# Normalised tokens of eleven chunks: written to DRAM as a high part, with the low part added there by a second transfer, in place of a sum formed on GpSimd

## The chip, the cores and the metric

The kernel runs as one program on one core of one Trainium2 chip. The metric is device time in microseconds (us): the median over timed runs. Engines are called by the names of the profile: PE is TensorE (matmuls), DVE VectorE, ACT ScalarE, POOL GpSimd, SP SyncE, which here only issues transfers. Each engine works through its own instructions strictly in the order of the program. They wait for each other by semaphores, and a waiting instruction holds up everything behind it on its engine.

## What is computed

Three stages, all in fp32. Attention over 8 x 8 heads of 576 tokens and 64 dimensions gives x (8 x 576 x 512). A layer norm and a two-layer MLP with a residual follow, then a mixing stage along channels and tokens. The change lies in what connects the first two:

```python
kv = np.einsum('bhsf,bhsd->bhfd', k_p, v)
num = np.einsum('bhsf,bhfd->bhsd', q_p, kv)
...
x = np.ascontiguousarray(attn_out.transpose(0, 2, 1, 3)).reshape(B, S, H * D)
xn = (x - mu) / np.sqrt(var + 1e-06) * g_ln
ch = np.maximum(xn @ w_ch1, 0.0) @ w_ch2        # 512 -> 2048 -> 512
x = x + ch
```

## The kernel before

**Split products.** A product in fp32 is made of three matmuls: each operand is cut into a high part, which PE takes as it is, and a low part, the rest (`mm3`, L73 to L76: L74 high by high, L75 low by high, L76 high by low). High parts are made on ACT (`hi_act`, L61), low parts on DVE (`lo_vec`, L64) or POOL (`lo_pool`, L67).

**Attention and the first MLP part run interleaved.** Attention is 16 units (4 pairs of batches by 4 pairs of heads). For a group of tokens of a unit PE projects keys or queries (`pj`), DVE takes the row maximum (`m`, L304) and subtracts it (`ys`, L306), PE turns the tile over (`tr`, L381), ACT takes exponentials (`pf`) and cuts the high part (`kph`, `qp`), DVE makes the low part of keys (`kpl`, L64), and POOL that of queries (`qp`, L67; in the last unit DVE). PE accumulates `kv` from `kph`, `kpl` and the values `vh`, `vl`, and makes the numerators `nm` from `qp` and `kv`. ACT copies them out (`num`, L420), PE turns them over (L433), and DVE divides (`rd`, L436 and L437; `xo`, L439) and collects the statistics of the norm (`lst`, L444). When the four units of a pair of batches are done, `ln_final` (L231 to L242) gives the mean and the factor of each token.

Finished tokens go through the first MLP part, `mlp_a`: 512 of the 2048 hidden features, in 18 chunks of 256 tokens. `tokens(ch)` loads the two tiles of 128 tokens (L507) and normalises each (`xn`, DVE L518). PE turns it over (L522), ACT cuts the high part `xh` and DVE the low part `xl`. POOL then adds the two to `xt` (L529), and SP stores `xt` to `xn_d[ch]` in DRAM (L530). PE goes on from `xh` and `xl`: 24 matmuls `ph<-xh,w` and `ph<-xl,w` (up, 128x256), ACT and DVE make the hidden tiles `hh`, `hl` (L206, L207), and 24 matmuls `ph<-w,hh` and `ph<-w,hl` (down, 128x512) end in a DVE sum with the residual (L557) and a store (L558). The later three quarters of the hidden features ("B" rounds, from 640 us on) read the normalised tokens back from `xn_d`.

A chunk is **wide** from the twelfth on (number 11; numbers begin at 0): attention is at its end by then, its PSUM tiles `nm` and `tr` are free for the transposes, ACT takes over the normalising (L516) and copies `xt` out of PSUM itself (L527). So POOL's sums stand in chunks 0 to 10 alone: 11 chunks, 22 sums of 128x512. `xn`, `xh`, `xl` and `xt` have one buffer each in these chunks, so the first tile of a chunk waits until the last reader of the chunk before is done. The second normalised tile of a chunk and the first of the next are made one behind the other.

**What sets the order.** The code is written as generators that are advanced in turn, with priorities for parts of it. A scheduler that keeps a simulated timeline then puts the instructions of each engine in a row: an instruction taken out or put in can shift the rows around it, and far from it. During the first two stages SP issues all transfers in one queue, in the order of the rows.

Of the kernel before, what the change touches and what calls it, by code (L numbers as in the profile page):

```python
# [9 lines left out]
F32 = mybir.dt.float32  # L10
# [5 lines left out]
ALU = mybir.AluOpType  # L16
# [4 lines left out]
P = 128  # L21
# [8 lines left out]
KC = DM // P  # L30
# [8 lines left out]
NC_ = CT * P  # L39
# [8 lines left out]
def f32(ap):  # L48
    return ap.bitcast(F32)
# [3 lines left out]
def body(ctx, tc, qT, kT, va, wbd, g, w1, w2, wth, wtok, wch, out):  # L53
    nc = tc.nc
    V, A, G, T, SY = nc.vector, nc.scalar, nc.gpsimd, nc.tensor, nc.sync
# [4 lines left out]
    def hi_act(dst, src):  # L60
        A.activation(dst, src, AF.Copy)  # L61

    def lo_vec(dst, src, hi):
        V.tensor_tensor(dst, src, f32(hi), op=ALU.subtract)  # L64
# [13 lines left out]
    def opened(*a, **kw):  # L78
        st = ExitStack()
        return st, st.enter_context(tc.tile_pool(*a, reuse_waits="tile", **kw))  # L80
# [4 lines left out]
    xn_d = [dram.tile([P, KC, NC_], F32, name=f"xnd{c}") for c in range(NCH)]  # L85
# [402 lines left out]
    def mlp_a(m):  # L488
        nonlocal chunk

        def wide(ch):
            return tail is not None and ch >= tail + WIDE

        def transposed(ch, i):
            if not wide(ch):
                return ps_ph.tile([P, KC, P], F32, name="ph")
            return (ps_tr if i % 2 else ps_nm).tile([P, KC, P], F32, name="tr" if i % 2 else "nm")

        def tokens(ch):
            x = []  # L500
            for i in range(CT):
                p, t = divmod(ch * CT + i, NT)
                if wide(ch) and ch % 3 == 1:
                    x.append(p_mt.tile([P, DM], F32, name=f"x{i}"))
                else:
                    x.append(p_ma.tile([P, DM], F32, name="x", bufs=XB))
                SY.dma_start(out=x[i], in_=x_d[p][:, t, :])  # L507
            pool = p_ma if not wide(ch) or ch % 2 else p_mt
            xh = pool.tile([P, KC, NC_], F32R, name="xh")
            xl = pool.tile([P, KC, NC_], F32R, name="xl")  # L510
            xt = p_ma.tile([P, KC, NC_], F32, name="xt")
            for i in range(CT):
                xn = p_ma.tile([P, DM], F32, name="xn")
                p, t = divmod(ch * CT + i, NT)
                if wide(ch):
                    A.activation(xn, x[i], AF.Identity, scale=ln_rs[p][:, t:t + 1], bias=ln_nb[p][:, t:t + 1])  # L516
                else:
                    V.tensor_scalar(xn, x[i], ln_mv[p][:, t, 0:1], ln_rs[p][:, t:t + 1], op0=ALU.subtract,  # L518
                                    op1=ALU.mult)
                tp = transposed(ch, i)  # L520
                for c in range(KC):
                    T.transpose(tp[:, c, :], xn[:, c * P:(c + 1) * P], ident)  # L522
                o = slice(i * P, (i + 1) * P)
                hi_act(xh[:, :, o], tp)
                lo_vec(xl[:, :, o], tp, xh[:, :, o])
                if wide(ch):
                    A.activation(xt[:, :, o], tp, AF.Copy)  # L527
                else:
                    G.tensor_tensor(xt[:, :, o], f32(xh[:, :, o]), f32(xl[:, :, o]), op=ALU.add)  # L529
            SY.dma_start(out=xn_d[ch], in_=xt)  # L530
            return x, xh, xl

        nxt = None
        for ch in range(NCH):
            if nxt is None:
                yield ch
                chunk = ch
                nxt = tokens(ch)
            x, xh, xl = nxt
            nxt = None  # L540
            yield -1
            hid = []
            for f in range(m.nf // 2):
                if wide(ch) and f % 2:
                    ph = ps_pj.tile([P, 2, NC_], F32, name="pj")
                else:
                    ph = ps_ph.tile([P, 2, NC_], F32, name="ph")
                m.up(f, ph, xh, xl)
                hid.append(m.relu(p_ma, ph))
                yield -1  # L550
                if f == 0 and ch + 1 < NCH and wide(ch):
                    nxt = tokens(ch + 1)
                    yield -1
            for i in range(CT):
                acc = ps_ph.tile([P, DM], F32, name="ph")
                m.down(i, acc, hid)
                V.tensor_tensor(x[i], acc, x[i], op=ALU.add)  # L557
                SY.dma_start(out=xp_d[ch][:, i, :], in_=x[i])  # L558
                yield -1
# [8 lines left out]
    done, msteps, p_ma, p_mt, need, tail, chunk = 0, 0, None, None, 0, None, 0  # L568
    for g in ga:
# [5 lines left out]
        if done >= nload:  # L575
            if p_ma is None:
                s_st.close()
                s_ma, p_ma = opened(name="ma", bufs=1, side="left")
# [74 lines left out]
    def load_b(ch, xt=None):  # L653
        if xt is None:
            xt = p_xb.tile([P, KC, 4 * P], F32, name="xt")
        for i in range(2):
            SY.dma_start(out=xt[:, :, i * NC_:(i + 1) * NC_], in_=xn_d[2 * ch + i])
        return xt
# [35 lines left out]
    xt = load_b(0, first[:, 0:4].rearrange("p k a c -> p k (a c)"))  # L694
# [458 lines left out]
    for r in range(2):  # L1153
        done = 0
        for ch in range(NQ):
# [7 lines left out]
            for n, m in enumerate(ms):  # L1163
# [9 lines left out]
                if r == 0 and ch == 0 and n == 1:  # L1173
                    xt = load_b(1)
# [4 lines left out]
                if n == len(ms) - 1 and not (r and last):  # L1179
# [5 lines left out]
                    if not (r and ch == NQ - 2):  # L1185
                        xt = load_b((ch + 2) % NQ)
# [204 lines left out]
```

## Time and profile before

| what | value |
|---|---|
| median of 3 runs | 1669.17 us (1665.57 to 1670.7) |
| the profiled execution | 1668.41 us |
| its span | 1666.6 us |
| PE busy | 1619.8 us (97%) |
| DVE busy | 1279.9 us (77%) |
| ACT busy | 876.3 us (53%) |
| POOL busy | 721.7 us (43%) |
| mean granted PE clock | 0.99 of full speed |

The profile is one execution. "Busy" is the time in which an engine had an instruction in work. A timeline row gives the start, the busy time, engine, line, operation, what is written from what, how many in a row, and in brackets the idle time ahead of it and what ended that. Matmuls overlap in the pipe, so the distance of their starts says more than the busy time of one: at full clock 0.119 us for 256 columns. The granted clock is given in shares of the full 2.4 GHz; half of it is the other level, 1.2 GHz. Idle time on an engine other than PE costs something only where PE ends up waiting for it.

### The profile page before, as it was taken

The page shows a single profiled execution, that of the slowest core. Times are in us where ns is not written, and L with a number is a line of the kernel's source. Part 1 is how long each engine was busy: PE and PEld are TensorE (multiplying, and loading weights), DVE is VectorE, ACT ScalarE, POOL GpSimd, SP SyncE. Part 2 cuts the span into 40 slices and gives each one's busy share as a digit, 9 for nine tenths or more (in the row PEclk, how much of TensorE's full clock was granted, in tenths as well). Part 3 has the DMA queues.
Part 4 walks back from the last instruction along what each step waited for, and adds up shares of the span by engine and source line. Part 5 has one row for each costly group of instructions (what it writes and reads, how often), then busy time and mean ns, then how long its engine had stood idle before and what let it go on. Part 6 is the DMA issues. An engine that isn't in the chain of part 4 may idle for free.

```text
span 1666.6 us, 29023 instructions
## 1 busy us (share of the span) xinstructions
PE 1619.8 (97%) x11080; PEld 1487.9 (89%) x11080; DVE 1279.9 (77%) x2277; ACT 876.3 (53%) x1715; POOL 721.7 (43%) x562
## 2 busy tenths in 40 slices
PE   8899999999999999999999999999998999999998
PEld 6777899999999888889899999998898899999998
DVE  7989878888987953778786676688666787888884
ACT  6777767677775652445453444444443444444441
POOL 7876988899981001222112222211322443344430
PEclk9999999999999999999999999999999999999999
DMA  5334333333322734455547444463257565865754
GB/s 190 102 95 126 110 96 105 114 111 109 112 77 88 243 123 152 150 173 194 191 166 267 168 154 153 135 226 129 87 209 281 176 233 207 279 216 206 241 201 178
DMA packets 120329, 273.81 MB, mean 164 GB/s; under 512 B 9088, under 2 KB 62720, under 8 KB 112768
## 3 DMA queue, kind: packets, MB, share of 16 engines
q1 hardware_dynamic: 119904, 270.93, 47.9%
q8 instruction: 87, 1.43, 0.3%
q10 hardware_dynamic: 288, 1.05, 0.2%
q14 instruction: 50, 0.41, 0.1%
HBM read 195.92 MB, written 73.92 MB: 162 GB/s over the span
## 4 chain that ended last, share of the span: by engine, by line
PE 83%; DVE 11%; issue 2%; DMA 2%; POOL 1%; ACT 1%; SPq 0%; DVEq 0%; ACTq 0%; POOLq 0%
PE acc L74 6%; PE acc L75 6%; PE acc L76 6%; PE ph L75 4%; PE ph L76 4%; PE ph L74 4%; PE pa L74 3%; PE pa L76 3%; PE pa L75 3%; PE mc L74 2%; PE mc L75 2%; PE mc L76 2%; PE pj L74 2%; PE ma L74 2%; PE ma L76 2%; PE ma L75 2%
## 5 line engine op out<-in xcount | busy, mean ns | idle before, releaser
L667 POOL TENSOR_TENSOR c<-xt 128x512 f32<-128x512 f32 x17 | 22.7, 1335 | 373.8 <-DMA xt<-xnd 273.4
L74 PE MATMUL acc<-wd,hb 128*128 128x512 f32 x432 | 170.2, 394 | 1.8 <-DVE xo L833 1.8
L75 PE MATMUL acc<-wd,hb 128*128 128x512 f32 x432 | 170.1, 394 | 0.0
L67 POOL TENSOR_TENSOR qp<-pf,qp 128x512 fp32r<-128x512 f32 (+1 forms) x120 | 147.8, 1255 | 13.4 <-ACT qp L61 12.8
L76 PE MATMUL acc<-wd,hb 128*128 128x512 f32 x432 | 152.6, 394 | 0.4 <-DVE hb L787 0.4
L304 DVE TENSOR_REDUCE m<-pj 128x4 f32<-128x512 f32 (+1 forms) x160 | 99.4, 625 | 40.0 <-PE pj L76 39.4
L64 DVE TENSOR_TENSOR kpl<-pf,kph 128x1024 fp32r<-128x1024 f32 (+1 forms) x67 | 100.6, 1501 | 11.1 <-ACT kph L61 10.8
L64 DVE TENSOR_TENSOR a<-zf,a 128x1024 fp32r<-128x1024 f32 (+1 forms) x57 | 97.7, 1724 | 12.0 <-ACT a L61 11.9
L306 DVE TENSOR_TENSOR ys<-pj,m 128x512 f32<-128x512 f32 (+1 forms) x160 | 99.6, 628 | 2.1 <-ACT qf L391 0.5
L316 ACT ACTIVATE pf<-ys 128x512 f32<-128x512 f32 (+1 forms) x160 | 85.3, 584 | 30.2 <-DVE ys L306 23.2
L61 ACT ACTIVATE a<-zf 128x1024 fp32r<-128x1024 f32 (+1 forms) x57 | 56.7, 1013 | 82.8 <-POOL zf L927 40.2
L74 PEld LDWEIGHTS acc<-wd,hb 128*128 128x128 f32 x432 | 81.7, 189 | 13.7 <-DVE xo L833 2.4
L75 PE MATMUL kv<-kpl,vh 128*65 128x256 f32 x300 | 86.2, 287 | 7.2 <-DVE kpl L64 7.2
L75 PEld LDWEIGHTS acc<-wd,hb 128*128 128x128 f32 x432 | 81.7, 189 | 10.9
L76 PEld LDWEIGHTS acc<-wd,hb 128*128 128x128 f32 x432 | 77.5, 189 | 13.0 <-DVE hb L787 1.1
L74 PE MATMUL kv<-kph,vh 128*65 128x256 f32 x300 | 86.4, 288 | 0.0
L76 PE MATMUL kv<-kph,vl 128*65 128x256 f32 x300 | 84.5, 282 | 0.0
L780 ACT ACTIVATE u<-pa 128x256 f32<-128x256 f32 x108 | 41.2, 382 | 71.1 <-PE pa L76 70.3
L1090 POOL TENSOR_SCALAR k<-k 128x512 f32<-128x512 f32 x31 | 27.5, 888 | 114.1 <-ACT k L1089 114.1
L420 ACT ACTIVATE num<-nm 65x288 f32<-65x288 f32 x128 | 50.6, 402 | 49.6 <-PE nm L76 42.5
L74 PE MATMUL ma<-t,a 128*128 128x288 f32 x248 | 74.5, 301 | 1.9 <-ACT a L61 1.9
L76 PE MATMUL ma<-t,a 128*128 128x288 f32 x248 | 73.7, 300 | 1.3 <-DVE a L64 1.3
(402 smaller groups left out, 6308.3 us busy)
## 6 DMA issues: line engine op xcount, KB each, us to landing
t<-wtkdt SPq DMA_DIRECT2D x16, 1440.0 KB, 7.3
t<-wtkd SPq DMA_DIRECT2D x15, 1440.0 KB, 6.2
t<-wtkdt SPq DMA_DIRECT2D x16, 1152.0 KB, 6.6
xt<-xnd SPq DMA_DIRECT2D x34, 512.0 KB, 5.0
raw<-in_w SPq DMA_DIRECT2D x32, 512.0 KB, 4.3
in<-in_va SPq DMA_DIRECT2D x30, 325.0 KB, 3.1
xd<-xo SPq DMA_DIRECT2D x48, 192.0 KB, 3.0
x<-xd SPq DMA_DIRECT2D x36, 256.0 KB, 3.0
```

The costliest lines, as they stand in the source:

```text
L61: A.activation(dst, src, AF.Copy)
L64: V.tensor_tensor(dst, src, f32(hi), op=ALU.subtract)
L67: G.tensor_tensor(dst, src, f32(hi), op=ALU.subtract)
L74: T.matmul(out_, lhsT=lh, rhs=rh, start=start, stop=False, **kw)
L75: T.matmul(out_, lhsT=lh, rhs=rl, start=False, stop=False, **kw)
L76: T.matmul(out_, lhsT=ll, rhs=rh, start=False, stop=stop, **kw)
L304: V.tensor_reduce(m[:, :2 * n], pv, axis=AX.X, op=ALU.max, apply_absolute_value=True)
L306: marks.append(V.tensor_tensor(ys[:, :2 * n, :], pv, m[:, :2 * n].unsqueeze(2).to_broadcast([P, 2 * n, NF]), op=ALU.subtract).ins)
L316: A.activation(kp[:, :2 * n, s, :], ys[:, :2 * n, :], AF.Exp, scale=sc)
L420: A.activation(self.num[:, h, o:o + 288], nm, AF.Copy)
L780: A.activation(t, ps, AF.Copy)
L1090: G.tensor_scalar(k, k, -MAGIC, 1.0, op0=ALU.add, op1=ALU.mult)
```

## The change

In chunks 0 to 10 the tile `xt` and its two POOL sums are gone. SP stores `xh` to `xn_d[ch]`, and POOL then issues a transfer of `xl` to the same place which adds to what lies there. The wide chunks keep `xt`. Lines behind the diff move by one to two (the residual sum is L559 then, the new store L531, the accumulating transfer L532).

```diff
-            xt = p_ma.tile([P, KC, NC_], F32, name="xt")
+            xt = p_ma.tile([P, KC, NC_], F32, name="xt") if wide(ch) else None
...
                 lo_vec(xl[:, :, o], tp, xh[:, :, o])
                 if wide(ch):
                     A.activation(xt[:, :, o], tp, AF.Copy)
-                else:
-                    G.tensor_tensor(xt[:, :, o], f32(xh[:, :, o]), f32(xl[:, :, o]), op=ALU.add)
-            SY.dma_start(out=xn_d[ch], in_=xt)
+            if wide(ch):
+                SY.dma_start(out=xn_d[ch], in_=xt)
+            else:
+                SY.dma_start(out=xn_d[ch], in_=f32(xh))
+                G.dma_start(out=xn_d[ch], in_=f32(xl), accum_op=ALU.add)
```

The accumulating transfer waits for the store (a semaphore of SP's queue, `DMAHW`) and for DVE's `xl`. The next chunk's `xh` waits for the store, and its first `xl` for the accumulating transfer (`DMASW`), since both read the one buffer. The loads of `xn_d` for the B rounds wait for it too.

The change also moves rows on all engines up to the end of the first MLP part, since the scheduler places them anew; from 640 us on the order is the same in both kernels. Three places follow.

**DVE, chunk 10, the last one ahead of the wide chunks.** The rows `xs` are the B rounds' first operands, made from `xn_d`; names in brackets are the semaphores waited for. Before:

```order
L518 TENSOR_SCALAR xn<-x,lmv,lrs 128x512 [waits DMAHW7_49,PE_49]
L242 SCALAR_TENSOR_TENSOR lnb<-lmv,lrs 128x9 [waits DVE_49]
L64 TENSOR_TENSOR xl<-ph,xh 128x4x128 [waits Activation_49]
L64 TENSOR_TENSOR xs<-xs 128x512 [waits DMAHW6_49,Activation_49]
L667 TENSOR_TENSOR xs<-xs 128x512 [waits DMAHW7_49]
L672 TENSOR_TENSOR xs<-xs 128x512
L64 TENSOR_TENSOR xs<-xs 128x512 [waits Activation_49]
L64 TENSOR_TENSOR xl<-ph,xh 128x4x128 [waits Activation_49]
```

After:

```order
L518 TENSOR_SCALAR xn<-x,lmv,lrs 128x512 [waits DMAHW5_49,PE_49]
L64 TENSOR_TENSOR xl<-ph,xh 128x4x128 [waits DMASW1_49,Activation_49]
L436 TENSOR_SCALAR rd<-kv 128x6 [waits PE_49]
L437 RECIPROCAL rd<-rd 128x6 [waits DVE_49]
L439 TENSOR_TENSOR xo<-kv,rd 128x384 [waits DMAHW2_49,DVE_49]
L64 TENSOR_TENSOR xl<-ph,xh 128x4x128 [waits Activation_49]
```

The `xs` rows stood between the two `xl` of the chunk; now they come behind the `xl` of chunk 11, and a short piece of a division stands there.

**PE, chunk 9.** Each row of four transposes `ph<-ident,xn` is one of the chunk's two tiles; `nm<-qp` are the last unit's numerators. Before:

```order
L433 MATMUL kv<-ident,num 128x65
L522 MATMUL ph<-ident,xn 128x128 x4
L433 MATMUL nm<-ident,num 128x65
L74 MATMUL nm<-qp_7606,kvh 65x288
L75 MATMUL nm<-qp_7607,kvh 65x288
L76 MATMUL nm<-qp_7606,kvl 65x288
...
L433 MATMUL kv<-ident,num 128x65
L522 MATMUL ph<-ident,xn 128x128 x4
```

After:

```order
L522 MATMUL ph<-ident,xn 128x128 [waits DVE_49]
L522 MATMUL ph<-ident,xn 128x128 x3
L381 MATMUL tr<-ident,ys 128x128 [waits PE_49,Activation_49]
L381 MATMUL tr<-ident,ys 128x128 x3
L433 MATMUL nm<-ident,num 128x65 [waits Activation_49]
L433 MATMUL nm<-ident,num 128x65 x5
L381 MATMUL tr<-ident,ys 128x128 [waits DVE_49,PE_49,Activation_49]
L381 MATMUL tr<-ident,ys 128x128 x3
L522 MATMUL ph<-ident,xn 128x128 [waits DVE_49]
L522 MATMUL ph<-ident,xn 128x128 x3
L355 MATMUL nm<-ident,kvs 128x65 [waits DVE_49]
L74 MATMUL ph<-xh,w_0_0_0_162 128x256 [waits DVE_49,Activation_49]
```

Before, six of the numerators stood between the two tiles and 18 more between the second tile and the second matmul of the up products. Now chunk 9 is brought ahead of the numerators, and transposes alone lie between its first tile and its up products.

**DVE, chunk 8.** Before:

```order
L518 TENSOR_SCALAR xn<-x,lmv,lrs 128x512
L436 TENSOR_SCALAR rd<-nm 128x6
L64 TENSOR_TENSOR xl<-ph,xh 128x4x128
L64 TENSOR_TENSOR kvl<-nm,kvh 128x260
L437 RECIPROCAL rd<-rd 128x6
L304 TENSOR_REDUCE m<-pj 128x4
L439 TENSOR_TENSOR xo<-nm,rd 128x384
L306 TENSOR_TENSOR ys<-pj,m 128x512
```

After:

```order
L64 TENSOR_TENSOR xl<-ph,xh 128x4x128
L437 RECIPROCAL rd<-rd 128x6
L439 TENSOR_TENSOR xo<-nm,rd 128x384
L304 TENSOR_REDUCE m<-pj 128x4
L444 BN_STATS lst<-xo 128x6 x3
L518 TENSOR_SCALAR xn<-x,lmv,lrs 128x512
L306 TENSOR_TENSOR ys<-pj,m 128x512
L436 TENSOR_SCALAR rd<-nm 128x6
L64 TENSOR_TENSOR kpl<-pf,kph 128x1024
L64 TENSOR_TENSOR xl<-ph,xh 128x4x128
```

The second form is nearly the one that chunk 1 has in both kernels, on DVE and on PE: a division, its statistics, both tiles of the norm and a `kpl` of 128x1024 lie in one run.

## Rows read from the trace of the kernel before

**Rows 1.** Windows: time, length, busy us of PE, PEld, DVE, ACT, POOL; clock, DMA.

```profile
350.00:400.00 50.00, 48.87 (x395) 47.14 (x394) 41.61 (x71) 36.86 (x70) 46.94 (x40) 1.00 0.34 101
...
500.00:560.00 60.00, 56.15 (x411) 52.48 (x410) 48.46 (x113) 30.53 (x57) 8.38 (x6) 0.94 0.43 146
```

**Rows 2.** Windows of 5 us at the two long stops of PE.

```profile
210.00:215.00 5.00, 5.00 (x27) 5.00 (x27) 4.71 (x11) 0.00 (x0) 5.00 (x7) 0.57 0.13 45
550.00:555.00 5.00, 3.84 (x18) 3.85 (x19) 5.00 (x7) 1.77 (x3) 1.67 (x1) 0.50 1.05 407
```

**Rows 3.** Waits of PE, 160 to 560 us: total us, times, longest.

```profile
PE kv L75 <- DVE kpl L64: 5.1, 5, 2.4
```

**Rows 4.** Groups of POOL, 160 to 560 us: busy us, mean ns of one, idle before.

```profile
L529 POOL TENSOR_TENSOR xt<-xh,xl 128x512 f32<-128x512 f32 x22 | 33.3, 1518 | 46.2 <-DVE xl L64 46.1
```

**Rows 5.** The store's line L530 (issue in ns, time to landing), and another transfer.

```profile
L530 SPq DMA_DIRECT2D xnd<-xt x18: 319/323/424, 168.5 to 636.3; - x18
DMA to landing us min/median/max: 2.6/2.7/5.5
...
wch<-wcd SPq DMA_DIRECT2D x4, 512.0 KB, 10.5
```

**Rows 6.** Timeline of PE, chunk 1.

```profile
205.84 0.36 PE L74 MATMUL ph<-xh,w 128*128 128x256 f32 x1 [0.61 <-DVE xl L64]
...
206.90 0.35 PE L74 MATMUL pj<-wb,kh 128*128 128x256 f32 x1 [0.70 <-DVE ys L306]
...
209.93 0.47 PE L75 MATMUL kv<-kpl,vh 128*65 128x256 f32 x1 [2.44 <-DVE kpl L64]
...
214.26 0.31 PE L75 MATMUL ph<-xl,w 128*128 128x256 f32 x1
```

**Rows 7.** Timeline of DVE, chunk 1.

```profile
198.33 1.84 DVE L64 TENSOR_TENSOR kpl<-pf,kph 128x1024 fp32r<-128x1024 f32 x1
...
200.70 0.67 DVE L557 TENSOR_TENSOR x<-ph,x 128x512 f32<-128x512 f32 x1
...
207.34 2.54 DVE L64 TENSOR_TENSOR kpl<-pf,kph 128x1024 fp32r<-128x1024 f32 x1
```

**Rows 8.** Timeline of PE, chunk 10.

```profile
546.18 0.66 PE L522 MATMUL ph<-ident,xn 128*128 128x128 f32 x4 [0.88 <-DVE xn L518]
547.92 0.39 PE L74 MATMUL ph<-xh,w 128*128 128x256 f32 x1 [1.08 <-ACT xh L61]
548.62 0.96 PE L522 MATMUL nm<-ident,xn 128*128 128x128 f32 x4 [0.32 <-ACT xn L516]
551.16 0.58 PE L75 MATMUL ph<-xl,w 128*128 128x256 f32 x1 [1.57 <-DVE xl L64]
```

**Rows 9.** Timeline of DVE, chunk 10.

```profile
546.89 1.80 DVE L64 TENSOR_TENSOR xs<-xs 128x512 fp32r<-128x512 f32 x1
...
550.43 0.68 DVE L64 TENSOR_TENSOR xl<-ph,xh 128x512 fp32r<-128x512 f32 x1
```

**Rows 10.** Durations: timelines of ACT and PE, and a group of DVE.

```profile
502.18 1.09 ACT L395 ACTIVATE pf<-tr 128x512 f32<-128x512 f32 x2 [0.63 <-PE tr L381]
...
504.20 1.05 ACT L61 ACTIVATE qp<-pf 128x1024 fp32r<-128x1024 f32 x1
...
506.09 0.60 ACT L61 ACTIVATE xh<-ph 128x512 fp32r<-128x512 f32 x1
...
528.18 0.61 PE L522 MATMUL ph<-ident,xn 128*128 128x128 f32 x4
...
L64 DVE TENSOR_TENSOR qp<-pf,qp 128x1024 fp32r<-128x1024 f32 x4 | 5.6, 1400 | 1.0 <-ACT qp L61 1.0
```

**Rows 11.** Timeline of PE, chunk 5.

```profile
381.80 0.34 PE L75 MATMUL kv<-kpl,vh 128*65 128x256 f32 x1 [1.13 <-DVE kpl L64]
```

**Rows 12.** Timelines of POOL and of SP, chunk 2.

```profile
257.31 2.57 POOL L67 TENSOR_TENSOR qp<-pf,qp 128x512 fp32r<-128x512 f32 x2 [0.41 <-DMA x<-xd]
...
256.93 0.32 SPq L530 DMA_DIRECT2D xnd<-xt  x1
```

## Prediction

> **What bounds the kernel now.** I read the page first (PE is busy 97% of the span), then PE by stages, then what PE waits for in the stage that the change touches, then the timelines at those waits. From 160 us to the end of the first MLP part at 640 us PE runs without a break except in short stops; the window of 350 to 400 us holds 1.13 us of them, that of 500 to 560 us 3.85 us [rows 1]. What ends PE's waits in this stage is DVE above all, `kpl` first [rows 3]; no wait of PE in the stage ends on POOL. So POOL's sums, 22 of them for 33.3 us [rows 4], are off the path. What the change can move is the two long stops, and others that a new order may make.
>
> Stop 1 is in chunk 1: 0.61 + 0.70 + 2.44 = 3.75 us idle, the last of it for a `kpl` that took 2.54 us [rows 6, 7]. After it PE is slow for a while: the granted clock of 210 to 215 us is 0.57, against 1.00 over a stretch like 350 to 400 us [rows 1]; half is the lower of its two levels, 1.2 GHz [rows 2]. Twenty matmuls from 209.93 to 214.26 us take 4.33 us [rows 6], where they would take 20 x 0.119 = 2.4 us at full clock: 1.9 us more. Together 5.65 us. Stop 2 is in chunk 10: 0.88 + 1.08 + 0.32 + 1.57 = 3.85 us idle [rows 8], and again a stretch at half clock, 0.50 [rows 2], for the 20 matmuls that follow; the same 1.9 us, together 5.75 us. Its reason is in DVE's queue: `xs` rows for the B rounds from 546.89 us stand ahead of the chunk's second `xl`, which runs at 550.43 us [rows 9].
>
> **What is removed.** The 22 sums leave POOL. Off the path they are worth nothing to PE directly: 0. They might help through DVE, whose `kpl` of 128x1024 took 1.84 and 2.54 us in one chunk [rows 7]; but POOL is busy for 46.94 of 50 us there [rows 1], with 22 sums in some 400 us, and other work moves into their places, so I put 0 here too and keep a gain for a rival below.
>
> **What is added.** Eleven accumulating transfers, issued by POOL. No row shows one. An issue of the store takes SP 0.32 us [rows 5]; the work it replaces took 2 x 1.518 = 3.04 us [rows 4]. I take an issue of about 1 us, nearer to the other issue than to the sums, which leaves POOL lighter by some 2 us a chunk. From issue to landing transfers of 512 KB took 2.6 us at the least and 10.5 us in the slowest group [rows 5]; I take about 3, and 10.5 as the bound. What waits on the landing is the next chunk's first `xl` on DVE, with all of DVE's queue behind it. Chunk 1 is at 206 us and chunk 10 at 547 us [rows 6, 8], so chunks lie some 38 us apart, so a landing of 10.5 us is hidden. Only chunk 10 is followed closely: there SP has the store, POOL nothing else left, and between chunk 10's `xl` and that of chunk 11 lie its 24 down products, 24 x 0.24 = 5.7 us (512 columns, twice the 0.119 us of 256), which start only when the up products and the hidden tiles are done. Store and accumulation of 2.7 + 3 us with two issues of 1 us and less fit there; at 10.5 us the transfer would show by 2 or 3 us. I take 0.
>
> The accumulating transfer also waits, at the head of POOL's queue, for its store on SP. Behind it stand the low parts of queries, keys and values for PE. In chunk 2 the store was issued at 256.93 us, behind other transfers of SP, and POOL's next `qp` began at 257.31 us [rows 12]; if that store is held as long after, it lands at 257 + 2.7 = 259.7 us at the latest and holds POOL 2.4 us at the most; with the sum no longer ahead of it, it can be issued up to 1.5 us sooner, which leaves about 1 us. PE never waited for POOL, so a late POOL of that size is hidden by what PE has queued. I take 0, with a rival for the other case.
>
> On "DMA: Bandwidth & Descriptors", section "Anatomy of one DMA — SWDGE (gpsimd) path", the Trainium skill fits 2.0 us plus bytes / 436 GB/s for a transfer from this queue: an estimate of 3.2 us for 512 KB, and the sum would be the same by it.
>
> **What is moved, and this decides.** The order of rows changes up to 640 us.
>
> *Chunk 10.* The `xs` rows are behind the `xl` of chunk 11, and SP's loads for them behind the store. Stop 2 loses its 1.57 us and the 0.88 us that fell to the queue ahead of `xn`; the turn of `xh` on ACT and of the first `xn` of chunk 11 stays as it was: 1.08 + 0.32 = 1.4 us [rows 8]. A stop of 1.4 us, like the one of 1.13 us in chunk 5 [rows 11] behind which the clock stayed at 1.00 [rows 1], brings no slow stretch. Gain 5.75 - 1.4 = 4.35 us. The `xs` work itself is needed only at 640 us, and has some 70 us of wide chunks for cover.
>
> *Chunk 9.* Its up products need both tiles' `xh` and `xl`. Counted from PE's first transposes: the first `xh` on ACT at 0.6 to 1.2 us [rows 10], then in ACT's row two `pf` (1.09), a `qp` (1.05), two `pf` (1.09) and only then the second `xh`, which ends at 1.2 + 1.09 + 1.05 + 1.09 + 0.6 = 5.05 us. The second `xl` follows on DVE (about 0.6 to 0.9 us, with a low part of `qp` of 1.4 us and an `xn` in the same row [rows 10]): 5.9 us or so. PE has until then six rows of small work: four groups of four transposes, four rows that keep PE 0.61 us with the pipe's end [rows 10] and about 0.45 us one behind the other, and ten smaller turns, six of numerators and four of `kvs`, about 0.75 us by the same measure: 2.5 us, an estimate. So PE stands for 5.9 - 2.5 = 3.4 us, and a stop like that was followed both times by a slow stretch of 1.9 us [rows 2]: 5.3 us. Before, 24 numerators of 0.13 us (288 columns; 3.2 us) covered this and there was no stop.
>
> *Chunk 8.* DVE's and PE's rows repeat those of chunk 1 almost one by one. Between the ends of its two `kpl` DVE worked without a break for 209.88 - 200.17 = 9.7 us in chunk 1 [rows 7], of which one residual sum (200.70 us, some 0.6 us) now comes earlier: 9.1 us. PE's rows between the two groups of `kv` that use them are the same as there. So the stop is that of chunk 1, 3.75 us, or 0.6 us less: 3.15; with the clock 5.05 to 5.65. I take 5.3. Before, chunk 8 had no stop. Stop 1 in chunk 1 stays: its rows are unchanged but for the sum.
>
> **Sum.** On the profiled execution: 1668.4 - 5.75 + 1.4 + 5.3 + 5.3 = 1674.7 us. The median is 0.8 us above the profiled one, so 1675.5 us on its footing; I say **1675 us**, 0.35% slower.
>
> **Rivals**, on the footing of the median:
>
> 1. *Only one of the two new stops is there, or neither brings the slow stretch.* DVE may enter chunk 8 with a lead, as in chunk 5, where a wait for `kpl` cost 1.13 us and no clock [rows 11]: 1675.5 - 5.3 + 1.1 = 1671.3 us; if it costs nothing 1670.2. The same for chunk 9 alone. For it: POOL is lighter, and an `xn` less late on DVE is enough to shorten the wait. Against it: the row order is the one that stopped before. Around 1670 us.
> 2. *DVE is relieved, and the order costs nothing (faster).* With the sums gone POOL reads less beside DVE; both new stops stay under 1 us, and stop 1 shrinks so far that its slow stretch goes: 1669.2 - 4.35 - 1.9 = 1663 us. For it: `kpl` of one size takes from 1.84 to 2.54 us beside a busy POOL [rows 7]. Against it: POOL's other work moves into the gaps. The Trainium skill, "SBUF — State Buffer", section on who interferes with whom, says that a DVE instruction with two inputs in SBUF is blocked by a GpSimd one that reads SBUF; the two durations agree with that.
> 3. *The accumulating transfer holds POOL (slower still).* If issue and wait for the store take longer than the sums, 3.0 us and the store's landing of up to 5.5 us [rows 5], POOL falls behind by 2 to 5 us a chunk and PE begins to wait for low parts; it decides from the point where POOL's slack is used up, in the stage's last chunks or where two `qp` stand behind the transfer, as in chunk 2 [rows 12]. One such stop of 3.5 us with its slow stretch, 5.4 us, comes on top: 1681 us. Against it: POOL had 46 us of idle time ahead of the sums [rows 4], in which it can wait. The Trainium skill names a mechanism on the same page, in the box on the "DVE blocks DMA" trap: while DVE runs certain copies and scalings GpSimd can't write the descriptors of its transfers. No row here shows it; it would lengthen the issue.
> 4. *The change does not do what it says:* POOL is no lighter, since issuing costs it as much as two sums. As POOL is not on the path, the time is that of the forecast or of rival 1, and no number changes.
>
> **How the numbers follow.** Forecast, both new stops with their slow stretches: 0.45, at 1673 to 1678 us. Rival 1: 0.32, at 1667 to 1673. Rival 2: 0.13, at 1660 to 1666. Rival 3: 0.10, at 1678 to 1686. A measurement of this kernel can tell about 0.3% from no change: below 1664.2 us is faster, above 1674.2 slower. Of the forecast two thirds lie above that and a third within; rival 1 is within; of rival 2 four fifths are faster; rival 3 is slower. Faster 0.11, same 0.48, slower 0.41. The range of 8 in 10 leaves out rival 2's lower half and rival 3's upper half: 1663 to 1681 us; the likeliest case has 1673 to 1678.
>
> **What would show it.** PE's timeline around chunk 10 without the wait for `xl` and with the clock at 1.00 there (the gain); a wait of over 3 us ahead of chunk 9's first `ph<-xh` or `ph<-xl`, ended by ACT `xh` or DVE `xl`; one ahead of `kv<-kpl` in chunk 8, with a granted clock near 0.5 behind each. POOL's row for an accumulating issue near 1 us, and no wait of PE on POOL. The forecast is wrong if the clock stays at 1.00 behind both new stops, if the accumulating transfers land so late that DVE's `xl` waits on them, or if PE waits on POOL.

## The result, and the profile after

The changed kernel takes 1692.06 us (median of 4 runs, 1687.78 to 1694.61) against 1668.47 us for the kernel before in the same comparison (4 runs, 1665.57 to 1670.7): a ratio of 1.0131, interval 1.0114 to 1.0149. It is slower, by 23.6 us where 5.8 were forecast, and the time lies 11 us above the range. The profiled execution of the changed kernel took 1687.78 us with a span of 1685.9 us, 19.3 us more than that of before; the other three runs are 3 to 7 us longer still.

At the same instruction PE was within about 1 us of the kernel before until 334 us, 15.9 us behind at 660 us, and 19.3 us behind at the end. So most of the loss is in the stage that was changed. PE's waits there (engine, line, what it waited for; total us, times, longest), to be held against [rows 3]:

```profile
PE kv L75 <- DVE kpl L64: 6.4, 4, 4.1
PE ph L75 <- DVE xl L64: 4.5, 4, 2.3
PE pj L75 <- DVE xl L64: 2.8, 1, 2.8
...
PE nm L75 <- POOL qp L67: 0.8, 1, 0.8
```

Rows of PE's timeline with its longest stops in chunks 5, 6, 8, 9, 10 and 11 (start, us, row, idle time before it and what ended it). Those of chunk 5 and chunk 10 (561.62 us) are to be held against [rows 8, 11]; the others had no such stop before:

```profile
390.69 0.47 PE L75 MATMUL kv<-kpl,vh 128*65 128x256 f32 x1 [4.08 <-DVE kpl L64]
...
425.60 0.39 PE L75 MATMUL ph<-xl,w 128*128 128x256 f32 x1 [2.25 <-DVE xl L64]
...
499.01 0.35 PE L74 MATMUL pj<-wb,kh 128*128 128x256 f32 x1 [1.03 <-DVE rd L436]
...
500.12 0.34 PE L75 MATMUL kv<-kpl,vh 128*65 128x256 f32 x1 [0.53 <-DVE kpl L64]
...
535.24 0.66 PE L381 MATMUL tr<-ident,ys 128*128 128x128 f32 x4 [0.86 <-ACT pf L395]
...
537.79 0.58 PE L74 MATMUL ph<-xh,w 128*128 128x256 f32 x1 [1.21 <-ACT xh L61]
539.47 0.58 PE L75 MATMUL ph<-xl,w 128*128 128x256 f32 x1 [1.10 <-DVE xl L64]
...
561.62 0.39 PE L74 MATMUL ph<-xh,w 128*128 128x256 f32 x1 [0.69 <-ACT xh L61]
...
577.87 0.39 PE L75 MATMUL pj<-xl,w 128*128 128x256 f32 x1 [2.80 <-DVE xl L64]
```

The granted clock behind these stops, in windows (time, length, busy us of PE, PEld, DVE, ACT, POOL; clock, DMA share, GB/s). The first two and the last follow the stops of chunks 5, 9 and 11; the third follows that of chunk 10:

```profile
390.70:394.00 3.30, 3.30 (x16) 3.30 (x17) 3.30 (x10) 2.34 (x4) 1.35 (x1) 0.52 0.00 0
538.00:543.00 5.00, 3.90 (x17) 3.61 (x18) 4.04 (x10) 0.96 (x2) 0.53 (x1) 0.50 0.59 197
562.00:567.00 5.00, 5.00 (x46) 5.00 (x46) 4.40 (x21) 1.69 (x3) 0.00 (x0) 1.00 0.73 231
577.00:582.00 5.00, 4.13 (x21) 4.11 (x22) 5.00 (x10) 4.32 (x8) 0.00 (x0) 0.66 0.79 312
```

Adding up, chunk by chunk, PE's idle time and what its matmuls lost behind it (their distance less that at full clock, 0.119 us for 256 columns) gives after minus before: chunk 0 +0.8, chunk 1 -1.6, chunk 5 +4.7, chunk 6 +1.6, chunk 7 +0.6, chunk 8 +2.0, chunk 9 +4.9, chunk 10 -5.1, chunk 11 +7.2: 15.1 of the 15.9 us. Chunks 9 and 10 are as forecast. Chunks 5, 6 and 11 were not forecast; 5 and 11 are the largest, and they are where the experiments look.

**Chunk 5.** PE waits for a `kpl` on DVE. That row, and POOL's rows beside it (the transfer, and the two at the end of the `kpl`):

```profile
382.75 7.88 DVE L64 TENSOR_TENSOR kpl<-pf,kph 128x1024 fp32r<-128x1024 f32 x1
```

```profile
380.05 0.87 POOL L532 DMA_DIRECT2D xnd<-xl  x1
...
388.67 0.88 POOL L58 TENSOR_SCALAR kh<-in 128x640 fp32r<-128x640 f32 x1
389.64 2.41 POOL L67 TENSOR_TENSOR kl<-in,kh 128x640 fp32r<-128x640 f32 x1
```

The `kpl` lasts 7.88 us, where one of this size took 1.84 and 2.54 us [rows 7]. POOL works without a gap to 389.55 us (388.67 + 0.88; then 0.09 us of gap), and `kpl` ends at 390.63 us, 1.08 us after that. POOL's transfer did not wait for its store here: it has no idle time ahead of it, and POOL had stood idle for PE until 365.78 us, 14 us earlier, so it carried no backlog from an older wait either:

```profile
365.78 0.74 POOL L58 TENSOR_SCALAR vh<-in 128x650 fp32r<-128x650 f32 x1 [3.47 <-PE kv L75]
```

**Chunk 11.** DVE, and behind it PE, waits for the accumulating transfer of chunk 10 (the first two rows are the timelines of POOL and DVE, the third the transfer's landing, min, median and max of 11):

```profile
567.14 0.86 POOL L532 DMA_DIRECT2D xnd<-xl  x1 [23.79 <-DVE hl L207]
...
576.53 0.69 DVE L64 TENSOR_TENSOR xl<-nm,xh 128x512 fp32r<-128x512 f32 x1 [6.55 <-DMA xnd<-xl]
...
DMA to landing us min/median/max: 5.1/5.8/9.3
```

The store before it was issued at 562.68 us. From there to 576.5 us it is 13.8 us. The window below shows the 16 DMA engines taken up fully in most of that time (DMA share 1.02):

```profile
567.00:577.00 10.00, 8.07 (x47) 6.88 (x45) 2.53 (x11) 3.31 (x6) 0.86 (x1) 1.00 1.02 294
```

### The profile page after: what moved, and what is told of

Same layout as the page of the kernel before. It is cut to its first block, busy times and chain, and to the rows that moved or that the text cites. A ratio compares the mean times of both kernels' runs of the same rounds, so it can differ in the third digit from the quotient of the medians.

```text
span 1685.9 us, 29032 instructions
## 1 busy us (share of the span) xinstructions
PE 1627.7 (97%) x11080; PEld 1492.7 (89%) x11080; DVE 1279.3 (76%) x2277; ACT 875.4 (52%) x1715; POOL 698.0 (41%) x551
## 3 DMA queue, kind: packets, MB, share of 16 engines
q10 hardware_dynamic: 288, 1.05, 0.2%
## 4 chain that ended last, share of the span: by engine, by line
PE 81%; DVE 12%; DMA 3%; issue 2%; POOL 2%; ACT 1%; SPq 0%; DVEq 0%; POOLq 0%; ACTq 0%
PE acc L76 6%; PE acc L74 6%; PE acc L75 6%; PE ph L75 3%; PE ph L74 3%; PE ph L76 3%; PE pa L74 3%; PE pa L76 3%; PE pa L75 3%; PE ma L76 2%; PE ma L74 2%; PE ma L75 2%; PE mc L74 2%; PE mc L76 2%; PE mc L75 2%
## 5 line engine op out<-in xcount | busy, mean ns | idle before, releaser
L67 POOL TENSOR_TENSOR qp<-pf,qp 128x512 fp32r<-128x512 f32 (+1 forms) x120 | 142.1, 1217 | 28.8 <-ACT qp L61 28.7
```

The lines of the kernel that those rows point to most:

```text
L67: G.tensor_tensor(dst, src, f32(hi), op=ALU.subtract)
```

## The experiments

Medians are given with their ratio to the kernel before on the same chip (1668.6 to 1669.1 us in these comparisons).

**First theory: the order of rows, or the transfers.** The order that PE follows is set by the scheduler, and two of the transfers turn it. `nine` has transfers in nine chunks and keeps the sums in 4 and 10, and PE's rows are those of before. `two` has the transfers only in 4 and 10, and its order is the changed one but for 66 rows. `sum10` is the changed kernel with the sum in chunk 10 alone. The edit of `nine` against the changed kernel (the other two differ in the condition: `not in (4, 10)`, and `== 10`):

```diff
-            xt = p_ma.tile([P, KC, NC_], F32, name="xt") if wide(ch) else None
+            xt = p_ma.tile([P, KC, NC_], F32, name="xt") if wide(ch) or ch in (4, 10) else None
...
-            if wide(ch):
+                elif ch in (4, 10):
+                    G.tensor_tensor(xt[:, :, o], f32(xh[:, :, o]), f32(xl[:, :, o]), op=ALU.add)
+            if wide(ch) or ch in (4, 10):
```

> Accumulating transfers in nine of the eleven chunks, the POOL sums kept in chunks 4 and 10 alone; PE's rows are then word for word those of before. Theory O (the moved rows cost the time): the kernel stays at before's time, 1668 us give or take 4, with stop 2 in chunk 10 still there and no stop of over 2 us in chunks 5, 6, 8 and 9. Theory T (the transfers themselves cost the time, by holding POOL, by their landing and at the port that POOL and DVE share): nine elevenths of the 23 us, so about 1687 us.

> Accumulating transfers in chunks 4 and 10 alone, POOL sums in the other nine; PE's rows are then those of the changed kernel but for 66 of them. Theory O: the time of the changed kernel, 1688 to 1692 us, with its stops in chunk 5 (4.1 us idle for kpl), 6, 9 and 11. Theory T: two elevenths of the 23 us plus the wait in chunk 11 for chunk 10's landing (2.8 us idle in the changed kernel, with the slow stretch behind it up to 6.7): 1672 to 1676 us.

> The changed kernel with POOL's sum and the old store in chunk 10 alone, in nearly the same order of rows. If chunk 11's stop (2.80 and 1.73 us idle and some 2 us of slow matmuls) comes from the landing of chunk 10's accumulating transfer, it goes, and 5 to 7 us are won: 1685 to 1687 us. If it comes from the order of rows, the time stays at 1692 us, and DVE's xl there waits for something else.

Measured: `nine` 1680.55 us, 1.0071 [1.0054, 1.0089]; `two` 1681.34 us, 1.0079 [1.0059, 1.0099]; `sum10` 1680.68 us, 1.0094 [1.0062, 1.0126]. Neither theory was met: `nine` and `two` lie between the two forecasts, and `sum10` is below both of its own. Half of the loss comes with PE's order of before, so the order of PE's rows is not the whole cause. The DVE row and the PE row of `nine` in chunk 2:

```profile
258.11 11.23 DVE L64 TENSOR_TENSOR kpl<-pf,kph 128x1024 fp32r<-128x1024 f32 x1
```

```profile
269.40 0.48 PE L75 MATMUL kv<-kpl,vh 128*65 128x256 f32 x1 [7.44 <-DVE kpl L64]
```

POOL issued its transfer there at 257.79 us and was busy to 268.27 us; `kpl` ended 1.07 us later. A second one, in chunk 7, lasted 7.06 us and cost PE 3.16 us. The two stops make 10.6 of `nine`'s 11.4 us. In `sum10` PE's stop of 2.80 us in chunk 11 is gone, and the profiled execution is 7.1 us shorter than that of the changed kernel; but two of its five runs took 1689 us, and the intervals overlap, so the price of chunk 10's transfer is read from the trace and not from the medians.

**Second theory: three costs, the order, the wait for the store, the adding.** `plain` has the changed order (but for some of PE's rows near 180 us), and POOL's transfer goes to a scratch area `xs_d`, declared besides, without adding, so that it waits for no store. `accprev` adds into the chunk before, whose store has long landed (chunk 0 into its own). `waitplain` transfers without adding into the same place, and waits for the store.

```diff
-                G.dma_start(out=xn_d[ch], in_=f32(xl), accum_op=ALU.add)
+                G.dma_start(out=xs_d[ch], in_=f32(xl))                                # plain
+                G.dma_start(out=xn_d[max(ch - 1, 0)], in_=f32(xl), accum_op=ALU.add)  # accprev
+                G.dma_start(out=xn_d[ch], in_=f32(xl))                                # waitplain
```

> The low parts go to a scratch tensor by a plain transfer of POOL's queue, which neither adds nor waits for the store (so they are missing from what the later rounds read back); PE's rows are word for word those of the changed kernel. If adding in DRAM and waiting for the store are what costs, the time falls to 1680 us or below and the landing from 5.8 us to about 3. If the order of rows costs, it stays above 1685 us: only the wait in chunk 11 (up to 6.7 us) and the POOL hold in chunk 0 (0.83 us) can go, and the kpl of 7.9 us in chunk 5 is there again.

> The changed kernel with each accumulating transfer directed at the chunk before, whose store has long landed, so that POOL does not wait for a store (the later rounds read wrong low parts). PE's rows are those of the changed kernel. If adding makes the long kpl, there are some of over 4 us, though perhaps in other chunks, and landings stay near 5.8 us: 1682 to 1692 us. If the wait for the store makes them, no kpl is over 3.5 us and the time is 1674 to 1678 us.

> The changed kernel with a plain transfer of the low parts to xn_d in place of the accumulating one (it overwrites the high parts, so the later rounds read low parts alone). All rows and all waits are those of the changed kernel; POOL waits for the store as there. If the wait for the store (POOL held for 6 us in chunk 2, a backlog behind it) makes the long kpl, they are here too: chunk 5 with 4 us idle, 1685 us or more. If adding makes them, they are gone and the time is that of the plain transfer to a scratch tensor, 1674 us, plus up to 3 us for the holds and for chunk 10's landing.

Measured: `plain` 1674.09 us, 1.0031 [1.0018, 1.0044]; `accprev` 1674.28 us, 1.0043 [1.0027, 1.006]; `waitplain` 1689.0 us, 1.0116 [1.0084, 1.0148]. The two that don't wait for the store lose 5 us, whether they add or not: that is the price of the order, near the 5.8 us forecast for the whole. The one that waits and doesn't add loses 20 us. So the wait, with the rows that it moves, makes about 15 us, and the adding itself too little to be told apart (1.0043 against 1.0031, 1.0131 against 1.0116, both overlapping). In `waitplain` the chain of events is the same again, in chunk 2: POOL is held 5.64 us for the store, works on without a gap to 280.79 us, and the `kpl` ends 1.09 us after that:

```profile
273.63 8.25 DVE L64 TENSOR_TENSOR kpl<-pf,kph 128x1024 fp32r<-128x1024 f32 x1 [1.73 <-ACT kph L61]
```

```profile
281.93 0.47 PE L75 MATMUL kv<-kpl,vh 128*65 128x256 f32 x1 [6.51 <-DVE kpl L64]
```

In chunk 5 the difference lies in the order of POOL's rows. `waitplain` has them as in the changed kernel. `accprev` has PE's rows of the changed kernel, but two transfers stand earlier on POOL, and a few rows of DVE and ACT are moved in chunk 11. The transfer of chunk 5 stands ahead of `qh` instead of behind it. POOL then has a gap of 0.08 us ahead of `ql`, between the transfer and the `kpl`, which takes 1.32 us:

```profile
377.39 0.85 POOL L532 DMA_DIRECT2D xnd<-xl  x1
378.04 1.08 POOL L58 TENSOR_SCALAR qh<-in 128x640 fp32r<-128x640 f32 x1
379.20 1.57 POOL L67 TENSOR_TENSOR ql<-in,qh 128x640 fp32r<-128x640 f32 x1
...
381.80 1.32 DVE L64 TENSOR_TENSOR kpl<-pf,kph 128x1024 fp32r<-128x1024 f32 x1
```

At the same row of PE the changed kernel is 0.9 us behind `accprev` at 360 us, 5.2 at 425 us, 4.2 at 560 us and 8.0 at 620 us: chunk 5 makes some 4 us of this, chunk 11 another 4 us. That the place of the transfer is what frees this `kpl` is read from the traces; no run moved the transfer alone.

**Third theory: behind the wait POOL has a backlog, and a `kpl` that starts in it gets no turn.** One transfer in the order of before, in chunk 2 (`only2`) or in chunk 10 (`only10`), and the one of chunk 2 directed at chunk 1's piece, which takes its wait away and leaves the rows of all engines in their places (`a2prev`). The condition in the edit above is `ch != 2`, `ch < 10` and `ch != 2`; `a2prev` has besides:

```diff
-                G.dma_start(out=xn_d[ch], in_=f32(xl), accum_op=ALU.add)
+                G.dma_start(out=xn_d[ch - 1], in_=f32(xl), accum_op=ALU.add)
```

> The accumulating transfer in chunk 2 alone, POOL sums everywhere else; all of PE's rows are those of before. Theory P (behind an accumulating transfer POOL's queued work runs without giving DVE a turn at the port they share, so that a kpl that comes then lasts until POOL runs dry): one kpl of 10 to 12 us in chunk 2, PE idle 7.4 us with 1.8 us of slow matmuls behind, so 1669 + 9 = 1678 us from this one transfer. Theory S (the 2 of 11 chunks that hurt do so by chance of many small delays, with POOL late by some us): under 2 us, 1669 to 1671 us.

> The accumulating transfer in chunk 10 alone; PE's rows are those of before up to chunk 9 and those of the changed kernel in their form from chunk 10 on, with the xs rows behind chunk 11's xl. By the forecast's reckoning stop 2 (5.75 us) shrinks to 1.4: a gain of 4.35 us. Against it stands the landing of 9 us which chunk 11's first xl waits for (6.5 us on DVE, on PE 2.8 and 1.7 us idle and 2 us slow). If both hold: 1669 - 4.4 + 6.5 = 1671 us, within 3 us of before.

> The kernel before, with the accumulating transfer in chunk 2 alone, as in the run with chunk 2 alone (1676.4 us against 1668.9), but added into the piece of chunk 1, whose store has landed some 40 us earlier: the same transfer from the same queue at the same place of the order, without its wait for the store (chunk 2's low parts are missing in what the later rounds read, and added to chunk 1's). Theory: the loss comes from the backlog that POOL works off without a gap behind that wait, during which a kpl on DVE gets no turn (11.55 us): without the wait POOL's run is short, every kpl stays under 3 us, PE has no stop of 7.8 us at 271 us, and the time is that of before, 1669 us, 1668 to 1670. Rival: a transfer issued by POOL among its sums is enough to shut DVE out, wait or no wait: a kpl of more than 5 us in chunk 2, a stop of PE of 3 us and more behind it, 1673 to 1677 us.

Measured: `only2` 1676.43 us, 1.0048 [1.0033, 1.0063]; `only10` 1666.91 us, 0.9988 [0.9979, 0.9997]; `a2prev` 1669.43 us, 1.0 [0.999, 1.0011]. The timelines of `only2` in chunk 2, of POOL, DVE and PE:

```profile
260.33 1.06 POOL L534 DMA_DIRECT2D xnd<-xl  x1 [5.87 <-DMA xnd<-xh]
...
264.40 0.87 POOL L58 TENSOR_SCALAR kh<-in 128x512 fp32r<-128x512 f32 x1
...
270.16 0.84 POOL L58 TENSOR_SCALAR qh<-in 128x512 fp32r<-128x512 f32 x1
```

```profile
260.53 11.55 DVE L64 TENSOR_TENSOR kpl<-pf,kph 128x1024 fp32r<-128x1024 f32 x1
```

```profile
272.14 0.48 PE L75 MATMUL kv<-kpl,vh 128*65 128x256 f32 x1 [7.76 <-DVE kpl L64]
```

and of `a2prev` at the same place, POOL and then DVE:

```profile
255.03 1.06 POOL L534 DMA_DIRECT2D xnd<-xl  x1 [0.94 <-DVE xl L64]
257.47 2.56 POOL L67 TENSOR_TENSOR qp<-pf,qp 128x512 fp32r<-128x512 f32 x2 [1.38 <-DMA x<-xd]
...
260.72 1.57 POOL L58 TENSOR_SCALAR kh<-in 128x512 fp32r<-128x512 f32 x1
```

```profile
260.17 1.64 DVE L64 TENSOR_TENSOR kpl<-pf,kph 128x1024 fp32r<-128x1024 f32 x1
```

`only10` came out 4 us below what was expected of it, and `a2prev` at the time of before. The same `kpl` starts at nearly the same time in both `only2` and `a2prev`, beside a busy POOL, and takes 11.55 us in the one and 1.64 us in the other. With the wait, POOL issues the transfer 5.3 us later and then works off what has gathered, without a gap, to 271.00 us; without it the transfer is out early, a gap of 1.38 us follows, and DVE gets its turn. POOL's own row says the same from its side: `kh` takes 0.87 us where DVE gets no turn, and 1.57 us where it does. One such row is the whole loss of `only2`: 7.76 us of idle time, against 7.6 us between the medians.

So in chunk 2 the wait is the cause. It is not the condition everywhere: the transfers ahead of the long `kpl` of chunk 5 (7.88 us in the changed kernel, 7.87 in `sum10`, 7.65 in `waitplain`) had no idle time ahead of them, that of chunk 7 of `nine` (7.06 us) 0.11 us. What all of these share with chunk 2 is a transfer inside an unbroken run of POOL's work and a `kpl` that starts behind it in that run. So the rival named for `a2prev`, a transfer among POOL's work is enough, wait or no wait, fell in chunk 2, where a gap followed, and is borne out in chunks 5 and 7. In the profiled execution of the changed kernel the `kpl` of chunk 2 began 0.07 us ahead of the transfer, and was not held up; in `only2`, `nine` and `waitplain` it began 0.20, 0.32 and 0.44 us behind it and took 11.55, 11.23 and 4.58 us. The two rows of the changed kernel:

```profile
258.96 0.89 POOL L532 DMA_DIRECT2D xnd<-xl  x1 [6.13 <-DMA xnd<-xh]
...
258.89 1.21 DVE L64 TENSOR_TENSOR kpl<-pf,kph 128x1024 fp32r<-128x1024 f32 x1
```

**A version that beats both.** By the runs so far the transfer costs nothing where POOL has a gap behind it. That is chunk 10, where POOL has no work left, and chunk 1, where the stop was shorter in the changed kernel. `k_110` has transfers in these two alone (`not in (1, 10)` in the first edit); `actst_two` also issues the store from ACT's queue.

```diff
-                SY.dma_start(out=xn_d[ch], in_=f32(xh))
+                A.dma_start(out=xn_d[ch], in_=f32(xh))
```

> The kernel before, with transfers in chunks 1 and 10 alone. Chunk 10 alone gave 0.9988 [0.9979, 0.9997]; in the changed kernel the stop of chunk 1 was 2.5 us against 3.75. PE's order up to chunk 9 is that of before, the tail that of the changed kernel. Theory that the two gains are separate and add: 1668.9 - 2 - 1.2 = 1665.7 us, ratio 0.998, with no kpl over 3 us. Rival 1: chunk 1's transfer waits for its store as chunk 2's did and a kpl behind it is shut out: a kpl of over 5 us in chunk 1 or 2, 1672 to 1676 us. Rival 2: the 1.2 us of chunk 1 belonged to the changed order elsewhere: stop 1 at 3.7 us again, 1667 us like chunk 10 alone.

> As the run before it in this call (transfers in chunks 1 and 10 alone), but the store of the high parts in those two chunks is issued from ACT's queue, right behind the copy that makes them, in place of SP's, where it stands behind loads. Theory that the store's late issue is what holds POOL: POOL's wait for the store shrinks to the landing of about 2.6 us behind the second xh, chunk 10's accumulating transfer is issued 1 to 2 us sooner and DVE's wait in chunk 11 (6.55 us in the changed kernel) is shorter by as much; ACT pays two issues of some 0.3 to 0.6 us. Time 1664 to 1667 us, no slower than its pair. Rival: ACT is on the path in chunks 1 and 10 (its pf and qp copies stand ahead of PE's transposes and products), and the issues there cost more than they give: 1668 to 1671 us.

Measured: `k_110` 1665.71 us, 0.9983 [0.997, 0.9996], against 1665.7 expected; `actst_two` 1666.42 us, 0.9988 [0.9978, 0.9998]. No `kpl` in either is over 2.92 us. The stop in chunk 1 of `k_110`, which was 2.44 us [rows 6], and DVE's wait in chunk 11 in `k_110` and then in `actst_two`:

```profile
209.41 0.48 PE L75 MATMUL kv<-kpl,vh 128*65 128x256 f32 x1 [1.22 <-DVE kpl L64]
```

```profile
562.48 0.69 DVE L64 TENSOR_TENSOR xl<-nm,xh 128x512 fp32r<-128x512 f32 x1 [1.55 <-DMA xnd<-xl]
```

```profile
561.97 0.69 DVE L64 TENSOR_TENSOR xl<-nm,xh 128x512 fp32r<-128x512 f32 x1 [0.60 <-DMA xnd<-xl]
```

The kernel is faster than before by 2.9 us, which is little: 0.17%. That the gains of two chunks add is not shown, since the intervals of `k_110`, `only10` and `actst_two` overlap. Nor is the gain of chunk 10 the one that was expected. In `only10` and `k_110` DVE's `xs` rows still stand between the two `xl` of chunk 10, not behind chunk 11's as the expectation of `only10` has it, and stop 2 is still there: 0.88 + 0.99 + 0.32 + 0.96 = 3.15 us in `k_110` against 3.85 us [rows 8], with the clock at 0.66 behind it (550 to 555 us).

```profile
545.61 0.66 PE L522 MATMUL ph<-ident,xn 128*128 128x128 f32 x4 [0.88 <-DVE xn L518]
547.26 0.38 PE L74 MATMUL ph<-xh,w 128*128 128x256 f32 x1 [0.99 <-ACT xh L61]
547.96 0.66 PE L522 MATMUL nm<-ident,xn 128*128 128x128 f32 x4 [0.32 <-ACT xn L516]
549.58 0.39 PE L75 MATMUL ph<-xl,w 128*128 128x256 f32 x1 [0.96 <-DVE xl L64]
```

What became shorter in both chunks are DVE's rows that began beside POOL's sum or its neighbours. The first `xs` row of chunk 10 took 1.80 us before [rows 9], where a sum of 1.26 us began 0.01 us ahead of it, and takes 0.69 us in `k_110`, where POOL does nothing; the `kpl` of chunk 1 took 2.54 us [rows 7] and takes 1.32 us. The sum of before and the `xs` row of `k_110`:

```profile
546.88 1.26 POOL L529 TENSOR_TENSOR xt<-xh,xl 128x512 f32<-128x512 f32 x1 [13.73 <-DVE xl L64]
```

```profile
546.24 0.69 DVE L64 TENSOR_TENSOR xs<-xs 128x512 fp32r<-128x512 f32 x1
```

In the trace of `only10` PE gains nothing on the kernel before between 540 and 600 us; where its 2 us come from was not found. The theory that the late issue of the store is what holds POOL fell: in `actst_two` it goes out at 546.92 us, in `k_110` from SP at 547.23 us, and POOL's transfer follows 7.9 and 8.4 us later. What takes the time there is the store's landing, up to 7.4 and 7.9 us in the two kernels, where the DMA engines' share is 0.97 (547 to 556 us in `k_110`).

## Why the prediction was wrong, point by point

- **The stop of chunk 10 goes: right.** Its idle time fell from 3.85 to 0.69 us with a clock of 1.00 behind it, a gain of 5.1 us where 4.35 were forecast.
- **The new stop of chunk 9: right.** 0.86 + 1.21 + 1.10 = 3.17 us of idle time against 3.4, and a slow stretch at 0.50. The second and third piece were ended by `xh` on ACT and `xl` on DVE as counted, the first by `pf` on ACT.
- **The new stop of chunk 8: too large.** 3.15 to 3.75 us with a slow stretch were taken from chunk 1. The trace has 1.03 us for `rd` and 0.53 us for `kpl`, 1.6 us, and PE lost 2.0 us there instead of 5.3. Rows that stand in the same order don't carry the same lead: this is what rival 1 said.
- **The stop of chunk 1 stays: half right.** It is 2.55 us instead of 3.75: its `kpl` took 1.32 us instead of 2.54 us [rows 7], beside other rows of POOL, since the sum ahead of them is gone.
- **The order as a whole: about right, in part by luck.** 5 us in `plain` and `accprev`, where hardly anything waits for a store. The sum without the transfers was +6.3 us. Chunk 8 cost 3.3 us less than forecast and chunk 1 won 1.6 us; a stop of 2.25 us in chunk 6, which the prediction did not have and which `plain` and `accprev` have too, took 1.6 us of that back.
- **Accumulating transfers at nothing, on POOL and in landing: wrong, and this is the failed term, 15 us or more by the medians.** In the profiled execution it is +4.7 us in chunk 5 and a good part of the +7.2 us in chunk 11. The issue, about 1 us, was right (0.88 us). POOL's lateness in chunk 2, up to 2.4 us, was right too: the `qp` behind the transfer began at 259.59 us where it began at 257.31 us [rows 12]. POOL stood 6.13 us for the store, but 3 us of these were the time that the sums had taken. What failed is the next step, "PE never waited for POOL, so a late POOL of that size is hidden by what PE has queued". The transfer doesn't reach PE through what POOL delivers (one wait, 0.8 us) but through DVE: where POOL works on without a gap behind it, a `kpl` on DVE that starts there waits for the end of that work. A wait for the store brings such a run about in chunk 2 of `only2`; in chunk 5 there was no wait at the transfer and no backlog from one, so what is left there is the place of the transfer among POOL's rows. Rival 3 had the wait for the store, but the wrong way to PE and 1681 us.
- **The sums' removal as a relief for DVE, rival 2: there, but outweighed.** `kpl` in chunk 1 and `xs` in chunk 10 of `k_110` became 1.2 and 1.1 us shorter, as the rival has it, so the sums were not worth 0: in chunk 10 one held up DVE inside stop 2. In the changed kernel the long `kpl` of 7.88 us stands against that, where the longest before was 2.54 us. The Trainium skill, "SBUF — State Buffer", section "SBUF: two separate sides" (the prediction cited another section of this page for the rival), says that of a DVE instruction with two inputs in SBUF and a GpSimd one that reads SBUF, the one that starts first gets the ports that they share "for the whole instruction" and the other waits. The trace before agrees: `xs` took 1.80 us behind a sum of 1.26 us, against 0.69 us without one. In `only2` the rule falls short: there DVE was shut out over a whole row of POOL's instructions (11.55 us), not over one.
- **The landing in chunk 10: mis-sized, and the second part of the failed term.** It was put at 0 for PE; DVE's `xl` in chunk 11 waited 6.55 us for it and PE 2.80 us for that `xl`, with a clock of 0.66 behind. An `xl` that waits for a late landing is among the signs that the prediction named for its being wrong. Some 4 us of chunk 11's loss are gone in `accprev`. Store and transfer were put at 2.7 + 3 us with two issues of 1 us and less, 7.7 us at the most, and took 13.8 us. The value was a median, while the DMA engines' share in that very stretch was 1.05 in the trace of before [rows 2], and was 1.02 in the trace after. The bound of 10.5 us was the row to take (9.3 us measured).
- **Two sums of the working.** The second `xh` of chunk 9 ends at 5.03 us, not 5.05, and the chances add up to 0.10 faster, 0.50 same and 0.40 slower, not 0.11, 0.48 and 0.41. Nothing follows from either.
- **What is open.** Why a transfer matters at all, and why 4 of 19 `kpl` behind one were not held to the end of POOL's run (last section). That other executions of the changed kernel are up to 7 us longer than the profiled one would fit such a stop of 6.5 to 7.8 us in chunk 2, but no trace of them exists, and it is not shown. Of the 19.3 us, 3.4 arose after 660 us and were not followed up.

## What to carry to other kernels

An engine that nobody waits for can still be the one that decides, if its work excludes another engine's: before putting a transfer or a wait into its queue, ask not only who waits for its results, but who runs beside the unbroken work that follows. Here an accumulating transfer must wait until its store has landed, and it did no harm where its engine had a gap behind it: with transfers in two such chunks of eleven alone the kernel was 0.17% faster than before. Price a landing by the DMA share of the stretch in which it falls, not by the median of its kind.

## What the runs showed of the hardware

- **DVE can be shut out by a row of POOL instructions behind a transfer.** Over 13 kernels with 53 `kpl` each from 150 us on, 15 lasted over 3 us, all in kernels with transfers from POOL. 14 of them started behind such a transfer inside an unbroken run of POOL's work (no gap over 0.05 us), and ended 1.07 to 1.10 us after that run ended, whether it had 2 instructions left or 10; the 15th (4.58 us, in `waitplain`) did not. In all, 19 `kpl` of 128x1024 started behind a transfer with over 1 us of such a run left; 15 waited for its end and 4 did not (1.84, 1.93, 1.98 and 4.58 us). Without a transfer ahead of them in the run, 380 of this size started, in all 13 traces, with over 3 us of it left, up to 25 us, and none took over 2.67 us. Why the transfer matters was not found.
- **An accumulating transfer takes longer than a plain one from the same queue.** Issue and landing of 11 transfers of 512 KB each, in `waitplain`, and the issue in the changed kernel, whose landing stands above:

```profile
L532 POOL DMA_DIRECT2D xnd<-xl x11: 537/592/775, 167.2 to 574.5; - x11
...
DMA to landing us min/median/max: 3.0/3.5/8.1
```

```profile
L532 POOL DMA_DIRECT2D xnd<-xl x11: 836/877/1067, 167.6 to 567.1; - x11
```

  0.59 us against 0.88 us for the issue, 3.5 against 5.8 us for the landing (median); in `plain` and `accprev`, without the wait, the landings are 4.2 and 5.7 us. The estimate of 3.2 us that the Trainium skill's fit gives ("DMA: Bandwidth & Descriptors", section "Anatomy of one DMA — SWDGE (gpsimd) path") is near the plain transfer and too short for the accumulating one.
- **Not every stop of over 2 us was followed by a lower clock.** Behind the stop of 2.25 us in chunk 6, and behind that of 1.03 us in chunk 8, the granted clock of the changed kernel was 1.00; behind those of chunks 5, 9 and 11 (4.08, 3.17 in three pieces, and 2.80 us) it was 0.52, 0.50 and 0.66, in the windows shown above:

```profile
425.60:430.60 5.00, 5.00 (x42) 5.00 (x43) 5.00 (x10) 2.70 (x4) 4.54 (x7) 1.00 0.38 69
...
499.00:504.00 5.00, 4.47 (x36) 4.27 (x37) 5.00 (x9) 2.16 (x3) 5.00 (x5) 1.00 0.06 21
```
